# Routing attention rows to eight experts: plain stores in token order and gathers by a table, instead of scatters into expert regions

## The chip, the cores and the metric

The kernel runs on one core of one Trainium2 chip. The core has five engines that run side by side, each with its own instruction queue: TensorE (PE in the profile; PEld is its weight load), VectorE (DVE), ScalarE (ACT), GpSimd (POOL) and SyncE (SP). Transfers between device memory (DRAM) and the on-chip memory are issued from the SP queue or from GpSimd's queue and carried by 16 DMA engines. The metric is device time of one launch in microseconds, lower is better. "The profiled execution" is one launch taken by the hardware profiler; all times of single instructions come from it.

## What is computed

First an attention over 8 batches and 8 heads (576 positions, 64 columns), a sum of a coarse part on positions averaged by four and a narrow local part; then a mixture of 8 experts over the 4608 rows that result, each row going to one expert.

```
out_up = np.repeat(sm_attn(q_d, k_d, v_d), 4, axis=2)     # q_d, k_d, v_d: means over 4 positions
mask = np.abs(pos[:, None] - pos[None, :]) < 4
out_local = softmax(where(mask, scale * q @ k.T, -1e9)) @ v
x = (out_up + out_local) as 4608 rows of 512

logits = x @ w_gate                        # 8 experts
e_idx = np.argmax(logits, axis=1)
gate_w = softmax(logits)[row, e_idx]
eom = sigmoid(x @ w_output_gate)
for e in range(8):
    mask = e_idx == e
    h = np.maximum(x[mask] @ w1[e], 0.0)   # 512 -> 1024
    ye = h @ w2[e]                         # 1024 -> 512
    out[mask] = gate_w[mask, None] * eom[mask, e, None] * ye
```

## The kernel before

**Attention and routing.** A unit is one batch and two heads; there are 32 units (NU), four per batch. Each unit is a set of small tasks: transposes and means of q and k (L382, L389, tasks Tq and Tk), coarse scores (L447, DS), local scores with a mask (L460, L470, LS), means of v (L425, VD), the products with v and the row sums (L493, V1; L503, V2; L515, V3), exponentials and logarithms on ScalarE, and on VectorE and GpSimd the division and the sum that give 128 columns of x, transposed (L538 to L559). TensorE uses its array in several shapes: 64 columns (T, DS), 64 x 64 quarters (LS, V1, V2, V3), 32 columns (VD, L591) and the whole array (L600, L623 to L629, L670).

After each batch, `gate(b)` routes its 576 rows, held as 6 columns (j) of 96 partitions: logits (L591, L600), the maximum and a one-hot of the expert (L610 to L617), the coefficient (L646 to L650), and the rank of the row among those of its expert (L623 to L629, matmuls with a triangular matrix and a running count `cum`). `pos` (L656 to L660) is expert region plus rank. L670 turns x back into rows, L674 copies them into `xh`, where each row also gets its coefficient and its token number (L650, L652). Then GpSimd scatters the rows, six indirect transfers per batch (L679), to row `pos` of `xs_dram`, which has a region of 4608 rows for each expert. The regions' first 640 rows are filled beforehand with a token number out of range (`prefill`, L697, SP queue).

The order of all these tasks on each engine is set by `Plan`: it goes through them with given durations, and among tasks that could start it takes the one with the smallest `10 * slot + AT[kind]`. The order that it gives is the order in the program; the chip then runs each queue in order.

**Experts.** Each expert takes up to 640 rows (CAPJ = 5 blocks of 128). For expert e: one plain load of its region into `xg` (L784, SP queue), 20 transposes (L750) and their evictions (L751), first products with w1 in 64 matmuls of 320 columns (L759, evicted by ScalarE, L762, and VectorE, L764), second products with w2 in 40 matmuls (L769), scaling by the coefficient that stands in the row (L771), and five scatters of 128 rows into `out`, with the token numbers read from the row (L772, GpSimd). xg, xgT, hs and y have two buffers each, the weights three. Weights of experts 0 to 2 are loaded during attention, those of expert 3 and later among the experts (L693, L694, GpSimd, 1 MB each as stored on chip). This part is written expert after expert, and a scheduler of the language puts it in order on each queue.

If an expert has more than 640 rows, a branch at the end (L789) works off the rest.

## Time and profile before

| | us |
|---|---|
| median of 3 runs | 519.19 (516.39 to 520.56) |
| the profiled execution | 523.01 |
| its span, first to last instruction | 520.9 |
| TensorE busy | 419.6 (81%) |
| ScalarE, VectorE, GpSimd busy | 199.2, 187.4, 177.2 |

The span is the time between the first and the last instruction in the profiled execution; about 2 us of that execution lie outside it. A busy share is a mean over stages that differ, so the rows below are taken by stage: attention with routing up to about 320 us, a passage to 342.6 us, the experts up to 510.5 us, and the end. The granted clock (PEclk) is the share of full speed that TensorE was given in a stretch. The page's list of transfers has 48 scatters into hx_xs, 40 into out_dram, eight prefills of 645 KB (5.8 us from issue to landing) and eight loads of xg of 645 KB (4.2 us).

### The profile page before, as it was taken

To read this page: it belongs to the slowest core of one execution; us is meant where nothing else is said; L and a number is where in the kernel's file an instruction comes from. 1 tells how busy PE (TensorE), PEld (TensorE's weight loads), DVE (VectorE), ACT (ScalarE), POOL (GpSimd) and SP (SyncE) were. 2 spreads that over 40 slices of the span, in tenths; PEclk is the share of its full clock that TensorE was granted. 3 is DMA by queue.
4 is the path that set the end of the run, shared out by engine and by line. 5 is a ranking of instruction groups with operands and counts; after the bars stand their busy time and mean duration, and the time that the engine had idled before them with its cause. 6 is when DMAs were issued, how large, how long until landed. Compare 5 with 4: busy or idle time off the path is not lost.

```text
span 520.9 us, 17550 instructions
## 1 busy us (share of the span) xinstructions
PE 419.6 (81%) x7849; PEld 304.6 (58%) x7849; DVE 187.4 (36%) x496; ACT 199.2 (38%) x449; POOL 177.2 (34%) x211
## 2 busy tenths in 40 slices
PE   3787878978897977987997966089959989999991
PEld 2666757656776765765776754065536646566550
DVE  5232443443463462443463453132213313223220
ACT  2243734553563552433463542023313332333331
POOL 6021522535434534424324453405221340512312
PEclk9986986997787895678697886579989997999997
DMA  8998799382992489272212010227893988873202
GB/s 130 178 194 210 172 213 170 75 124 65 173 170 72 80 135 200 53 119 58 60 43 55 18 34 16 78 69 167 133 259 79 202 165 176 198 158 123 91 24 76
DMA packets 85269, 62.74 MB, mean 120 GB/s; under 512 B 49597, under 2 KB 77245, under 8 KB 85184
## 3 DMA queue, kind: packets, MB, share of 16 engines
q0 software_dynamic: 30624, 40.43, 40.6%
q1 hardware_dynamic: 54560, 21.10, 17.9%
q8 instruction: 63, 1.03, 0.8%
q14 instruction: 22, 0.18, 0.1%
HBM read 68.23 MB, written 20.53 MB: 170 GB/s over the span
## 4 chain that ended last, share of the span: by engine, by line
PE 48%; issue 31%; POOL 8%; DMA 4%; ACT 3%; DVE 2%; another core or an unknown queue 2%; POOLq 1%; SPq 0%; DVEq 0%
PE T L389 9%; PE PD L493 7%; POOL out_dram L772 7%; PE T L382 5%; PE PL L515 5%; PE T L425 4%; PE PD L503 4%; PE T L591 3%; PE T L670 3%; DMA qk<-in_k_dram 2%; PE pu L759 2%; PE S L460 2%; PE S L447 2%; PE py L769 1%
## 5 line engine op out<-in xcount | busy, mean ns | idle before, releaser
L759 PE MATMUL pu<-xgT,w 128*128 128x320 f16 x512 | 75.1, 310 | 1.8 <-DVE xgT L751 1.2
L556 POOL TENSOR_TENSOR xT<-xl,xd 128x576 f32<-128x576 f32 x32 | 38.8, 1212 | 102.1 <-DVE xl L549 101.9
L769 PE MATMUL py<-w,hs 128*128 128x512 f16 x320 | 70.4, 379 | 0.0
L679 POOL DMA_INDIRECT hx_xs<-xh,g_pos x48 | 45.1, 939 | 70.1 <-DVE g_pos L660 24.8
L389 PE MATMUL T<-idq,qk 72*64 72x88 f16 (+1 forms) x1024 | 63.0, 312 | 6.3 <-issue 5.9
L759 PEld LDWEIGHTS <-w 128*128 128x128 f16 x512 | 51.8, 101 | 24.5 <-issue 2.9
L772 POOL DMA_INDIRECT out_dram<-y,xg x40 | 39.2, 979 | 64.0 <-ACT y L771 60.2
L762 ACT ACTIVATE hs<-pu 128x320 f16<-128x320 f32 x64 | 28.0, 437 | 83.3 <-PE pu L759 77.7
L389 PEld LDWEIGHTS <-qk 72*64 72x64 f16 x1024 | 47.5, 166 | 9.2 <-issue 9.2
L769 PEld LDWEIGHTS <-hs 128*128 128x128 f16 x320 | 31.3, 98 | 36.4
L764 DVE TENSOR_SCALAR hs<-pu 128x320 f16<-128x320 f32 x64 | 31.4, 491 | 45.7 <-PE pu L759 37.2
L382 PE MATMUL T<-id,qk 72*64 72x72 f16 x1024 | 35.4, 221 | 14.5 <-DMA qk<-in_q_dram 8.9
L493 PE MATMUL PD<-e,vd 64*64 64x72 f32 (+1 forms) x512 | 42.3, 317 | 5.7 <-issue 3.1
L771 ACT ACTIVATE y<-py,xg 128x512 f32<-128x512 f32 x40 | 27.5, 687 | 47.9 <-PE py L769 47.9
L397 DVE COPY kT<-T 128x576 f16<-128x576 f16 x32 | 24.2, 757 | 56.2 <-ACT kd L411 26.5
L493 PE MATMUL PD<-e,on_d 64*64 64x72 f32 (+1 forms) x512 | 42.2, 318 | 2.6 <-issue 2.6
L751 DVE COPY xgT<-tp 128x1024 f16<-128x1024 f16 (+1 forms) x24 | 13.2, 596 | 84.1 <-PE py L769 42.9
L523 ACT ACTIVATE r<-PD 128x582 f32<-128x582 f32 x32 | 21.0, 656 | 57.5 <-PE PD L503 41.6
L397 DVE COPY qT<-T 128x576 f16<-128x576 f16 x32 | 24.2, 757 | 50.9 <-PE T L389 39.2
L493 PEld LDWEIGHTS PD<-e,vd 64*64 64x64 f32 x512 | 36.2, 173 | 9.4 <-issue 8.6
L382 PEld LDWEIGHTS <-qk 72*64 72x64 f16 x1024 | 28.0, 130 | 23.4 <-issue 9.1
L515 PE MATMUL PL<-e,v 64*64 64x57 f32 (+1 forms) x1280 | 33.1, 252 | 10.0 <-issue 9.1
(109 smaller groups left out, 605.8 us busy)
## 6 DMA issues: line engine op xcount, KB each, us to landing
w<-in_moe_w_dram POOLq DMA_DIRECT2D x16, 1024.0 KB
v<-in_v_dram SPq DMA_DIRECT2D x128, 80.0 KB, 4.8
hx_xs<-zt SPq DMA_DIRECT2D x8, 645.0 KB, 5.8
xg<-hx_xs SPq DMA_DIRECT2D x8, 645.0 KB, 4.2
qk<-in_q_dram POOLq DMA_DIRECT2D x7, 576.0 KB
qk<-in_k_dram POOLq DMA_DIRECT2D x7, 576.0 KB
hx_xs<-xh,g_pos POOLq DMA_INDIRECT x48
out_dram<-y,xg POOLq DMA_INDIRECT x40
```

What stands on the lines that cost most here:

```text
L382: nc.tensor.transpose(t16[64 * h:64 * h + 64, HB * c:HB * c + HB], src.tile[:, 2 * hp + h, D * c:D * c + D], id16[0:HB, 0:HB])
L389: nc.tensor.matmul(_ap(o, [o.ap[0], [2, w]]), lhsT=src.tile[:, 2 * hp + h, D * (4 * a + m):D * (4 * a + m) + D], rhs=idq[:, 0:w], start=(a ...
L397: nc.vector.tensor_copy(xT.tile.rearrange("p (n c) -> p n c", c=8), T.tile.bitcast(F16)[:, 0:S].rearrange("p (c n) -> p n c", c=8))
L493: nc.tensor.matmul(p[o:o + 64, h, WC + q0:WC + q0 + c1 - c0], lhsT=w[r, blk, :], rhs=et[r, i, WC + c0:WC + c1], start=(blk == 0), stop=(bl ...
L515: nc.tensor.matmul(p[64 * h:64 * h + 64, par, c0:c1], lhsT=vbuf.tile[r, g, h, :], rhs=et[r, h, c0:c1], start=(g == 0), stop=True, skip_gro ...
L556: nc.gpsimd.tensor_tensor(xT.tile[:, hp, :].rearrange("p (n m) -> p n m", m=4), xl.tile.rearrange("p (n m) -> p n m", m=4), _bc(xd.tile, 4 ...
L679: ins = nc.gpsimd.indirect_dma_start(out=xs_dram.ap(), out_offset=bass.IndirectOffsetOnAxis(ap=pos.tile[:, j:j + 1], axis=0), in_=xh.tile[ ...
L759: nc.tensor.matmul(pu[:, 0:c1 - c0], lhsT=w1sb[:, c, 128 * f:128 * f + 128], rhs=xgT[:, c, c0:c1], start=(c == 0), stop=(c == 3))
L762: nc.scalar.activation(hs[:, f, c0:c1], pu[:, 0:c1 - c0], AF.Relu)
L764: nc.vector.tensor_scalar_max(hs[:, f, c0:c1], pu[:, 0:c1 - c0], 0.0)
L769: nc.tensor.matmul(py, lhsT=hs[:, f, 128 * j:128 * j + 128], rhs=w2sb[:, f, :], start=(f == 0), stop=(f == NG - 1))
L772: ins = nc.gpsimd.indirect_dma_start(out=out_rows, out_offset=bass.IndirectOffsetOnAxis(ap=xgi[:, j, Dm // 2 + 1:Dm // 2 + 2], axis=0), in ...
```

## The change

Rows of x, 514 numbers wide now (512 and the coefficient), are stored in token order, one plain store per batch from the SP queue; the scatters by GpSimd and the prefills are gone. What is to stand where is worked out instead in a table of 128 partitions by 40 columns (8 experts of 5 blocks): VectorE splits `pos` into the lane (low seven bits) and the block, makes a one-hot of each by comparing (`olo`, 128 wide, and `ohi`, 40 wide), multiplies the second by the token number plus one, and six matmuls per batch (task INV) sum the products, so that each token number arrives at its place; VectorE adds that to `acc`, with 576 times the batch added where something arrived. At the end `gidx` is the list to gather by (row 0 where the table is empty) and `sidx` the list to scatter by (out of range where it is empty).

Each expert's rows come by five gathers of 128 rows (GpSimd) into xg, which has three buffers. The experts' part is written in the order in which it is to run: gathers two experts ahead, the transposes for the next expert between the second products of this one, weight loads behind the scatters. The table AT is rewritten, and so are the durations of several tasks and one constant that the plan goes by.

```diff
 AT = {
-    "v": -31.38, "Tq": -3.33, "Tk": 1.99, "evq": -4.73, "evk": 4.65, "qd": -21.49, "kd": -8.83, "VD": 15.17,
+    "v": -56.99, "Tq": -8.95, "Tk": 2.82, "evq": -2.96, "evk": 9.62, "qd": 31.01, "kd": 38.57, "VD": 14.38,
...
-    xs_dram = nc.dram_tensor("hx_xs", (E * REG, XW // 2), I32, kind="Internal")
+    xs_dram = nc.dram_tensor("hx_xs", (N, XW // 2), I32, kind="Internal")
+    gpool = ctx.enter_context(tc.tile_pool(name="gpool", bufs=3))
...
-        tv = add("VD", n, "PE", 0.46, fn, deps=vt + [t_pv], uses=[T, vbuf], mode=32, lat=0.2)
+        tv = add("VD", n, "PE", 0.65, fn, deps=vt + [t_pv], uses=[T, vbuf], mode=32, lat=0.2)
...
-            exti = xh.tile[:, :, Dm:XW].bitcast(I32)
-            nc.vector.tensor_scalar(exti[:, :, 1], tok_i[0:P], scalar1=float(S * b), scalar2=None, op0=ALU.add)
...
-            nc.vector.tensor_scalar(m9.tile, m9.tile, scalar1=1.0, scalar2=float(REG), op0=ALU.subtract, op1=ALU.mult)
-            nc.vector.tensor_tensor(pos.tile, m9.tile, rsel.tile, op=ALU.add)
+            pos = posall[:, b, :]
+            nc.vector.scalar_tensor_tensor(pos, in0=m9.tile, scalar=float(REG), in1=rsel.tile, op0=ALU.mult, op1=ALU.add)
+            nc.vector.tensor_scalar(bk.tile, pos, scalar1=7, scalar2=None, op0=ALU.arith_shift_right)
+            nc.vector.tensor_scalar(lo.tile, pos, scalar1=127, scalar2=None, op0=ALU.bitwise_and)
...
+            nc.vector.tensor_tensor(ohi.tile, _ap(colv, [[colv.ap[0][0], P], [0, NJ], [1, NC]]), _bc(bk.tile, NC),
+                                    op=ALU.is_equal)
+            nc.vector.tensor_tensor(hit.tile, ohi.tile, _bc(tokv[0:P], NC), op=ALU.mult)
...
+            nc.vector.tensor_tensor(olo.tile, _ap(lane, [[lane.ap[0][0], P], [0, NJ], [1, 128]]), _bc(lo.tile, 128),
+                                    op=ALU.is_equal)
...
+            for j in range(NJ):
+                nc.tensor.matmul(G.tile[:, 0:NC], lhsT=olo.tile[:, j, :], rhs=hit.tile[:, j, :], start=(j == 0),
+                                 stop=(j == NJ - 1), skip_group_check=True)
...
+            g = G.tile[:, 0:NC]
+            if b:
+                nc.vector.tensor_scalar(g1.tile, g, scalar1=0.5, scalar2=float(S * b), op0=ALU.is_ge, op1=ALU.mult)
+            nc.vector.tensor_tensor(acc, acc, g, op=ALU.add)
+            if b:
+                nc.vector.tensor_tensor(acc, acc, g1.tile, op=ALU.add)
...
-        for j in range(NJ):
-            def fn(j=j):
-                ins = nc.gpsimd.indirect_dma_start(
-                    out=xs_dram.ap(), out_offset=bass.IndirectOffsetOnAxis(ap=pos.tile[:, j:j + 1], axis=0),
-                    in_=xh.tile[:, j, :].bitcast(I32), in_offset=None, bounds_check=E * REG - 1, oob_is_err=False)
...
+            nc.sync.dma_start(xs_dram.ap()[S * b:S * b + S, :].rearrange("(j p) d -> p j d", p=P),
+                              xh.tile.bitcast(I32))
...
-    for r in range(E):
-        add("pre", 2 * r + 1, "SP", 0.8, lambda r=r: prefill(r), deps=[t_cg])
...
+    def gather(xg, nj, idx, c0):
+        for j in range(nj):
+            nc.gpsimd.indirect_dma_start(
+                out=xg[:, j, :], out_offset=None, in_=xs_dram.ap(),
+                in_offset=bass.IndirectOffsetOnAxis(ap=idx[:, c0 + j:c0 + j + 1], axis=0),
+                bounds_check=N - 1, oob_is_err=False)
...
+        for e in range(E):
+            w1sb, w2sb = wts[e]
+            xgT, hs, y = xts[e]
+            if e + 2 < E:
+                fetch(e + 2)
+            up(xgT, hs, CAPJ, w1sb)
+            if e + 1 < E:
+                xts[e + 1] = tiles(CAPJ)
+            for j in range(CAPJ):
+                col = CAPJ * (E - 1 - e) + j
+                down(xgs[e], hs, y, j, w2sb, sidx[:, col:col + 1], True)
+                if e + 1 < E and 2 * j < CAPJ:
+                    turn(xgs[e + 1], xts[e + 1][0], CAPJ, 2 * j)
+            if e + 3 < E:
+                weights(e + 3)
```

Here `up` is the first products with their evictions, `down` one block's second products with scaling and scatter, `turn` the transposes of two blocks with their eviction, `fetch` five gathers.

What this makes of the queues is seen at three places. GpSimd's queue before, from the last batch's scatters (L679) through experts 0 and 1 (w: weight loads, L772: scatters into out):

```order
L679 DMA hx_xs<-xh_91,g_pos 36864x258 x6
L693 DMA w_7638<-in_moe_w_dram 128x4x1024
L772 DMA out_dram<-y,xg 4608x512 x4
L694 DMA w_7639<-in_moe_w_dram 128x8x512
L772 DMA out_dram<-y,xg 4608x512
L693 DMA w_7834<-in_moe_w_dram 128x4x1024
L772 DMA out_dram<-y,xg 4608x512 x4
```

and after, from the end of attention (L778: gathers, of experts 0 to 2 first, then of 3 and 4; L811: scatters):

```order
L778 DMA xg<-hx_xs,gidx 128x257 x15
L811 DMA out_dram<-y,sidx 4608x512 x5
L730 DMA w_7344<-in_moe_w_dram 128x4x1024
L731 DMA w_7345<-in_moe_w_dram 128x8x512
L778 DMA xg<-hx_xs,gidx 128x257 x5
L811 DMA out_dram<-y,sidx 4608x512 x5
L730 DMA w_7554<-in_moe_w_dram 128x4x1024
```

The loads of w1 moved from ahead of the scatters to behind them, and the gathers now stand in this queue, behind two weight loads. VectorE's queue in the last batch's routing, before, from the second copy of xh on:

```order
L674 COPY xh_91<-T 96x2x512
L646 TENSOR_REDUCE g_se<-g_eg 96x6
L647 TENSOR_SCALAR g_se<-g_se 96x6
L648 SCALAR_TENSOR_TENSOR g_den<-g_ez,g_se 96x6
L650 RECIPROCAL xh_91<-g_den 96x6
L652 TENSOR_SCALAR xh_91<-tok_i 96x6
L656 TENSOR_TENSOR g_rke<-g_oh,T 96x48
L658 TENSOR_REDUCE g_rsel<-g_rke 96x6
L659 TENSOR_SCALAR g_m_6986<-g_m_6986 96x6
L660 TENSOR_TENSOR g_pos<-g_m_6986,g_rsel 96x6
```

and after, from the same copy (now with the third) to the lookup and the coefficient:

```order
L714 COPY xh_100<-T 96x2x512 x2
L668 TENSOR_TENSOR g_rke<-g_oh,T 96x48
L670 TENSOR_REDUCE g_rsel<-g_rke 96x6
L672 SCALAR_TENSOR_TENSOR posall<-g_m_6994,g_rsel 96x6
L673 TENSOR_SCALAR g_bk<-posall 96x6
L674 TENSOR_SCALAR g_lo<-posall 96x6
L684 TENSOR_TENSOR g_olo<-lane,g_lo 96x768
L678 TENSOR_TENSOR g_ohi<-colv,g_bk 96x240
L680 TENSOR_TENSOR g_hit<-g_ohi,tokv 96x240
```

Both copies now stand ahead of the rank (L668), and the coefficient (L660 to L664 of the new file) comes behind these rows. The SP queue before, with the prefills among the loads of v:

```order
L360 DMA v<-in_v_dram 64x5x64 x20
L697 DMA hx_xs<-zt 128x5x258 x2
L360 DMA v<-in_v_dram 64x5x64 x4
L316 DMA wg<-in_moe_w_gate_dram 128x4x8
L317 DMA wg<-in_moe_w_output_gate_dram 128x4x8
```

and after, with the stores of the first two batches (L719):

```order
L373 DMA v<-in_v_dram 64x5x64 x34
L719 DMA hx_xs<-xh_99 96x6x257
L373 DMA v<-in_v_dram 64x5x64 x16
L719 DMA hx_xs<-xh_100 96x6x257
L373 DMA v<-in_v_dram 64x5x64 x16
```

The prefills are gone, and each store stands between loads of v. On TensorE, where the rows are too many to show, neighbouring task groups of different array shape follow each other at 194 places of attention before and at 164 after, the six matmuls of INV counted in.

## Rows read from the trace of the kernel before

**Rows 1.** Stages: us, busy us (instructions) by engine, granted clock, DMA share, GB/s
```profile
18.00:320.00 302.00, 251.00 (x6710) 200.61 (x6707) 129.58 (x345) 139.96 (x336) 114.22 (x124) 0.81 0.59 113
320.00:342.60 22.60, 6.97 (x60) 5.62 (x58) 6.96 (x29) 0.77 (x3) 6.04 (x7) 0.58 0.29 85
342.60:510.50 167.90, 155.37 (x972) 92.99 (x971) 43.29 (x86) 54.77 (x103) 46.71 (x49) 0.95 0.64 141
```

**Rows 2.** Waits in attention: engine line <- releaser: total us, times, longest
```profile
POOL xT L556 <- DVE xl L549: 101.9, 19, 11.6
PE T L425 <- issue: 11.9, 18, 2.4
PEld L460 <- issue: 3.8, 15, 0.7
PE PD L493 <- DVE xd L538: 2.5, 1, 2.5
PE T L425 <- ACT vd L431: 0.2, 1, 0.2
PE T L670 <- issue: 0.2, 1, 0.2
```

**Rows 3.** Timeline of PE: experts 5, 6, 7: start, us, line, [wait before]
```profile
454.38 8.85 PE L759 MATMUL pu<-xgT,w 128*128 128x320 f16 x64 [0.21 <-DMA out_dram<-y,xg]
463.07 8.80 PE L769 MATMUL py<-w,hs 128*128 128x512 f16 x40
471.70 1.06 PE L750 MATMUL tp<-id,xg 128*128 128x128 f16 x16
473.09 0.38 PE L750 MATMUL tp<-id,xg 128*128 128x128 f16 x4 [0.34 <-DVE xgT L751]
473.69 8.85 PE L759 MATMUL pu<-xgT,w 128*128 128x320 f16 x64 [0.21 <-DVE xgT L751]
...
501.69 8.80 PE L769 MATMUL py<-w,hs 128*128 128x512 f16 x40
```

**Rows 4.** Timeline of PE: starts of experts 0, 2 and 4
```profile
342.64 9.86 PE L759 MATMUL pu<-xgT,w 128*128 128x320 f16 x64 [0.21 <-DVE xgT L751]
...
386.62 2.40 PE L750 MATMUL tp<-id,xg 128*128 128x128 f16 x20 [6.17 <-DMA xg<-hx_xs]
...
430.67 2.40 PE L750 MATMUL tp<-id,xg 128*128 128x128 f16 x20 [3.01 <-DMA xg<-hx_xs]
```

**Rows 5.** Waits of the SP queue, all of the span
```profile
SPq L784 <- DMA out_dram<-y,xg: 112.7, 8, 27.9
```

**Rows 6.** Timeline of POOL: weight loads among the scatters of expert 0
```profile
352.80 0.82 POOL L693 DMA_DIRECT2D w<-in_moe_w_dram  x1 [19.16 <-PE pu L759]
...
361.44 0.93 POOL L694 DMA_DIRECT2D w<-in_moe_w_dram  x1
```

**Rows 7.** Stages by 20 us: one of the last experts
```profile
480.00:500.00 20.00, 19.45 (x131) 11.87 (x130) 5.83 (x12) 7.23 (x14) 4.86 (x5) 1.00 0.16 60
```

**Rows 8.** Chain that ended last, 326 to 343 us: start, us, what
```profile
326.15 0.16 DVE g_pos L660
...
332.73 2.37 DMA hx_xs<-xh,g_pos
...
335.69 4.18 DMA xg<-hx_xs
```

**Rows 9.** Timeline 318 to 345 us: rank matmuls, one scatter of rows
```profile
324.93 0.37 PE L626 MATMUL T<-g_oh,ones 96*96 96x40 f16 x5
...
331.51 0.92 POOL L679 DMA_INDIRECT hx_xs<-xh,g_pos  x1 [0.30 <-issue]
```

**Rows 10.** All scatters of L679 and L772: ns shortest/median/longest, first and last start
```profile
L679 POOL DMA_INDIRECT hx_xs<-xh,g_pos x48: 915/921/1050, 88.0 to 332.7; - x48
L772 POOL DMA_INDIRECT out_dram<-y,xg x40: 966/972/1016, 355.8 to 511.5; - x40
```

**Rows 11.** Groups by line and shape: busy us, mean ns
```profile
L545 DVE TENSOR_TENSOR xl<-PL,r 128x570 f32<-128x570 f32 x32 | 24.0, 749 | 0.7
```

More of the change, by code (lines that the diff above doesn't have):

```diff
@@ L70 @@
     SWITCH = 0.13
[L71 removed]
+    NEAR = 0.15
     def __init__(self, at):
@@ L392, in fn @@
                                              skip_group_check=True)
[L393 removed]
+            tp = add("T" + nm, n, "PE", 0.88, fn, deps=loads + [t_id, t_idq], uses=[T, src], mode=64, lat=0.16)
             xT = d[nm + "T"] = Buf(r_qT if i == 0 else r_kT)
@@ L764, in experts @@
                     nc.vector.tensor_scalar_max(hs[:, f, c0:c1], pu[:, 0:c1 - c0], 0.0)
-        y = sbF.tile([128, CAPJ, Dm], F32, tag="y")
-        for j in range(nj):
-            py = psF.tile([128, Dm], F32, tag="Y", bufs=2)
-            for f in range(NG):
-                nc.tensor.matmul(py, lhsT=hs[:, f, 128 * j:128 * j + 128], rhs=w2sb[:, f, :],
-                                 start=(f == 0), stop=(f == NG - 1))
-            nc.scalar.activation(y[:, j, :], py, AF.Copy, scale=coef[:, j, 0:1])
-            ins = nc.gpsimd.indirect_dma_start(
-                out=out_rows, out_offset=bass.IndirectOffsetOnAxis(ap=xgi[:, j, Dm // 2 + 1:Dm // 2 + 2], axis=0),
-                in_=y[:, j, :], in_offset=None, bounds_check=N - 1, oob_is_err=False)
-            if group:
-                tc.declare_no_dep(ins.ins, group="out_scatter", reason="the rows differ")
-                tc.add_to_no_dep_group("out_scatter", ins.ins)
@@ L779, with down @@
-    for e in range(E):
-        if e not in wts:
-            weights(e)
-        base = (E - 1 - e) * REG
-        xg = sbF.tile([128, CAPJ, XW // 2], I32, tag="xg")
-        nc.sync.dma_start(xg, xs_dram.ap()[base:base + 128 * CAPJ, :].rearrange("(j p) d -> p j d", p=128))
-        experts(xg, CAPJ, *wts[e], True)
+    def down(xg, hs, y, j, w2sb, idx, group):
+        py = psF.tile([128, Dm], F32, tag="Y", name="Y", bufs=2)
+        for f in range(NG):
+            nc.tensor.matmul(py, lhsT=hs[:, f, 128 * j:128 * j + 128], rhs=w2sb[:, f, :],
+                             start=(f == 0), stop=(f == NG - 1))
+        nc.scalar.activation(y[:, j, :], py, AF.Copy, scale=xg[:, j, Dm // 2:XW // 2].bitcast(F32))
+        ins = nc.gpsimd.indirect_dma_start(
+            out=out, out_offset=bass.IndirectOffsetOnAxis(ap=idx, axis=0),
+            in_=y[:, j, :], in_offset=None, bounds_check=N - 1, oob_is_err=False)
+        if group:
+            tc.declare_no_dep(ins.ins, group="out_scatter", reason="the rows differ")
+            tc.add_to_no_dep_group("out_scatter", ins.ins)
@@ new lines, in tiles, with fetch @@
+    def tiles(nj):
+        return (sbF.tile([128, 4, 128 * nj], F16, tag="xgT", name="xgT"),
+                sbF.tile([128, NG, 128 * nj], F16, tag="hs", name="hs"),
+                sbF.tile([128, nj, Dm], F32, tag="y", name="y"))
+    with tc.manual_schedule():
+        xgs, xts = {}, {}
+        def fetch(e):
+            xgs[e] = gpool.tile([128, CAPJ, XW // 2], I32, tag="xg", name="xg")
+            gather(xgs[e], CAPJ, gidx, CAPJ * (E - 1 - e))
+        fetch(0)
+        fetch(1)
+        count()
+        xts[0] = tiles(CAPJ)
+        for j0 in range(0, CAPJ, 2):
+            turn(xgs[0], xts[0][0], CAPJ, j0)
+        for e in range(E):
[13 more added lines that the diff above has]
+                weights(e + 3)
```

128 lines of the change are left out of this document (78 added, 50 removed), and 12 rows, old and new, of the table AT.

## The prediction

> **What bounds the kernel now.** The page's first line (TensorE 81% busy) mixes stages, so the first view to read is the table by stage [rows 1]. Up to 320 us (attention, routing) TensorE is busy 251.0 of 302 us at a mean granted clock of 0.81, a mixture of its two levels 1.2 and 2.4 GHz. From 320 to 342.6 us it does 7 us of work in 22.6: the gap between the last head and the first expert. From 342.6 to 510.5 us eight experts run, TensorE busy 155 of 168 us. Then come 10.4 us of last scatter and end of program, up to the span of 520.9, in which nothing is changed.
>
> The second view is what TensorE waited for in attention [rows 2]. Ten of its rows, from 11.9 down to 0.2 us, end with "issue", time with no releaser in the profile; they sum to 41.7 us, and the change adds or removes few matmuls there. Six rows, from 2.5 down to 0.2 us, are waits for another engine's data; they sum to 8.6 us. So a better order can win little by shorter waits for data, and VectorE and GpSimd (129.6 and 114.2 us busy in 302 us, [rows 1]) have room.
>
> The third view is TensorE's timeline among the experts. An undisturbed expert takes 19.31 us [rows 3]: the first products start at 454.38, the second at 463.07 (8.69 later), the next expert's transposes at 471.70 (8.63), its first product at 473.69 (1.99). Three experts are not like that [rows 4]: expert 2 starts after 6.17 us and expert 4 after 3.01 us of waiting for its xg, and after a pause the first products run slower: those of expert 0 show 9.86 us busy, an undisturbed expert's 8.85. Why xg is late stands in the waits of the SP queue [rows 5]: its loads waited 112.7 us for scatters into out_dram, one of them 27.9 us, since a scatter reads its token numbers out of the xg buffer and so holds it until it has landed. On GpSimd's queue the scatters come behind a 1 MB weight load issued early, right after the first products [rows 6].
>
> **The change, part by part.** The sum is made against the profiled execution, 523.01 us; the median of the runs shown is 519.19, 3.8 less, and I take that off at the end.
>
> *Experts.* Three buffers for xg, coefficients taken from xg but token numbers from a constant table (sidx), weight loads behind the scatters, and transposes for the next expert written between the second products. So the two waits go, with the slow clock behind them, and so do the 0.34 and 0.21 us for evictions between transposes and products. What stays per expert is 8.69 + 8.63 and the transposes' own 1.06 + 0.38 = 1.44 us: 18.76 us. Expert 0 still starts after a pause, 9.86 - 8.85 = 1.01 us more, so 19.77; expert 7 has no successor to transpose: 17.32, and 0.17 until its last matmul ends at 510.49. Sum 19.77 + 6 x 18.76 + 17.32 + 0.17 = 149.8 us against 510.49 - 342.64 = 167.85: **18.0 us less**. This needs cover: the next expert's rows must have landed when its transposes come up. Those for expert e+3 are issued when expert e+1 begins, behind two weight loads on the same queue, and the first are wanted one expert and one first product later, 18.8 + 8.7 + 1.7 = 29 us after. The whole stage moves as many bytes as before, and the 16 DMA engines were busy 0.64 of 167.9 us = 107 us [rows 1]; the last experts, which only scatter, show 0.16 x 20 = 3.2 us each [rows 7]. Taking 8 x 3.2 and about 2.5 us for each of seven loads of xg off (an estimate, below its 4.18 us from issue to landing, [rows 8]) leaves some 13 us per pair of weights. So 13 + 2.5 of transfers lie ahead of 29 us: covered, though one period's transfers (13 + 3.2 + 2.5 = 18.7) fill it almost wholly. If the cover is gone, the old waits return; lower bound of the gain about 6 us.
>
> *Gathers instead of one load.* 40 gathers on GpSimd, not measured. Nearest rows are the scatters of rows of the same length, 0.92 us and 0.30 us of issue between them [rows 9], and the wider ones at 0.97 [rows 10]. I take 1.22 us each. Per expert GpSimd then has 5 x 1.22 + 5 x 1.27 + 0.82 + 0.93 = 14.2 of 18.8 us [rows 6, 9, 10]: hidden. Removed with no gain on the path: 48 scatters (48 x 0.92 = 44 us of GpSimd, which stood idle 101.9 us for xl alone, [rows 2, 10]) and eight prefills of 645 KB, which nothing waited for.
>
> *From last head to first product.* Now [rows 8]: routing ends at 326.3, six scatters until 332.73, landing 2.37, load 4.18, transposes, first product at 342.64. After, VectorE makes two copies of xh ahead of the rank instead of one and the small operations of the coefficient behind it, so the rank multiply stays near 325.6. From there: four small operations to the split place, 1.0 us, 326.6; the lookup's three comparisons and products. For those the nearest row is the two-input operation of 570 columns at 749 ns [rows 11], 1.31 ns a column: 768 columns 1.0 us, 240 columns 0.32 us twice, so 328.3. Six small operations at 0.22 finish the coefficient at 329.7, when SP can issue the plain store; meanwhile the six matmuls and the table sum are done by about 330.6, so the store is the later one. Its landing lies between 2.37 (scatter) and 4.18 us (xg load of 645 KB; the store has 592 KB), I take 4.2: gathers from 334.0, the fifth issued at 338.9, landed 341.3 by the scatter's 2.37, four transposes, first product at about 341.9. That is **0.7 us less**; ends -2.5 (store 2.4) and +3 (gathers landing like the xg load, store slower).
>
> *Attention.* VectorE gets per batch 1.0 + 0.63 + 0.16 (place split, one operation folded) + 0.5 (table sum) - 0.16 (token numbers) = 2.1 us, eight times 17 us, on 129.6 of 302 us; TensorE gets eight groups of six narrow matmuls, which by five of the rank matmuls (0.37 us, [rows 9]) cost some 0.5 us a group, 4 us. The rewritten order has 164 instead of 194 places where neighbouring matmul groups use the array in another shape; the nearest row is L460 behind such a place, 3.8 us in 15 = 0.25 us [rows 2], part of which is issue that any place has. Half of it, 0.12 x 30 = 3.7 us, cancels the 4 us. **0**, with ends -12 (all of 30 x 0.25 = 7.5 and the 8.6 us of data waits, less 4) and +10 (half of the additions on the path). The store on SP stands ahead of loads of v for heads some units later, which wait for their buffers longer than for it: 0.
>
> Sum 523.0 - 18.0 - 0.7 + 0 = 504.3; less 3.8: **500.5 us**.
>
> **Rivals.** (1) *Attention shrinks too.* The new order and the freed GpSimd and queues take the -12: 488.5. For it: the waits and shape changes above are real rows. Against: the issue waits dwarf them.
>
> (2) *The lookup lies on the path.* 8 x (2.1 + 0.5) = 21 us back: 521, no change. Against it: VectorE is 57% idle in attention and the lookup's result is needed only at the end.
>
> (3) *Gathers behind weights.* Before, xg came over SP's queue; now it shares GpSimd's with 2 MB of weights per expert. By the Trainium skill, page "DMA: Bandwidth & Descriptors", section "SWDGE vs HWDGE vs iDMA", there is a single queue for transfers that GpSimd issues, and each DMA engine alternates between that one and the one fed by SP. The scatters held back up to 27.9 us [rows 5] look like that; no row here shows a gather behind a weight load. If the share of 18.7 us per period falls short by 3 us in each of the five periods, the queue lags 15 us, more than the 13 us of slack, and pauses of the old size come back from expert 5 or 6 on, 9 us with their clock: 510.
>
> (4) *GpSimd becomes the bound*, the slower case: a gather reads scattered rows of DRAM and might cost more than a scatter. Per expert GpSimd would need 5 x 1.27 + 1.75 = 8.1 us and five gathers; the gain is gone and 1% lost when 8 experts take 173.6 us, 21.7 each, from 2.7 us per gather on. At 3 us: 8 x 23.1 = 185, 536 us. Against: 88 indirect transfers in the trace, of two widths, all take 0.92 to 1.05 us [rows 10].
>
> That the overflow branch is entered can be excluded: the trace has 40 scatters at L772, eight times five, none from a branch, and counts don't change.
>
> **Numbers.** Forecast with its own range 494 to 507: 0.60; (1) 0.17; (3) 0.11; (2) 0.07; (4) 0.05. A measurement here tells about 1% from no change, 5.2 us. Faster (below 514): forecast, (1), (3), about 0.88; same 0.07; slower 0.05. The range leaves out the deeper part of (1), and (2) and (4): 487 to 511.
>
> **What would show it.** In the table by stage of the changed kernel, the experts should take about 150 us at clock 1.00 after the first, an expert 18.8 us on TensorE's timeline with no wait for DMA; a gather's row should read 0.9 to 1.0 us; the first product should start some 22 us after the last head; up to there about 320 us. I am wrong if waits for gathers stand before transposes (3), if GpSimd is over 0.95 busy among the experts (4), or if the last head ends more than 10 us from 320 (1, 2).

## The result and the profile after

The changed kernel takes **483.33 us** (median of 4 runs, 482.45 to 485.67) against 519.88 us before (4 runs, 516.39 to 520.58): ratio 0.930, interval 0.924 to 0.936. The prediction was 500.5 us with a range of 487 to 511. The sign was right, the gain was twice the forecast. Ratios with their intervals, here and below, compare only runs in the faster of two states that a program is seen in, while medians are over all runs, so a ratio is not always the quotient of the medians beside it; the profiled executions of runs a4, d1 and f1 were in the slower state, 4 to 6 us over their medians, and stages read from them are upper bounds.

The table by stage of the changed kernel, cut where its own last head (the end of the last sum on GpSimd that gives columns of x, L569, old L556) and first product lie (columns as in [rows 1]):

```profile
18.00:290.30 272.30, 219.56 (x6675) 182.20 (x6675) 153.88 (x383) 138.36 (x334) 79.41 (x81) 0.86 0.59 106
290.30:313.90 23.60, 8.11 (x67) 5.90 (x68) 9.42 (x37) 0.77 (x3) 7.79 (x8) 0.50 0.22 61
313.90:471.30 157.40, 151.99 (x974) 90.93 (x972) 44.46 (x86) 54.71 (x104) 81.89 (x83) 0.97 0.66 155
```

The last head ends at 290.29 instead of 319.78, the first product starts at 313.90 instead of 342.64, the last product ends at 469.62 instead of 510.49, the span at 481.64 instead of 520.93. So of 39.3 us, **29.5 went in attention**, which was forecast at 0; the passage grew by 0.7, the experts lost 12.1 (forecast 18.0), and the end, from last product to span, grew by 1.6.

What TensorE waits for in the changed kernel's attention, to be read against [rows 2]:

```profile
PE T L402 <- issue: 9.2, 4, 4.4
PE PL L528 <- issue: 6.9, 4, 3.2
PE T L690 <- DVE qT L410: 6.5, 5, 1.6
PE S L483 <- issue: 5.0, 2, 4.4
PE T L605 <- ACT kd L424: 2.2, 3, 0.7
PE T L690 <- DVE g_hit L680: 1.8, 1, 1.8
PE T L438 <- issue: 1.2, 2, 0.7
```

L438 is the old L425, the means of v: its "issue" waits were the largest row of before, 11.9 us in 18, and are now 1.2 in 2. Eight issue rows sum to 33.3 us (41.7 before), nine for data of another engine to 17.4 (8.6 before). All rows together are 50.7 us, 50.3 before: the list of waits shows nothing of the 29.5 us. They are in TensorE's busy time, 219.6 us instead of 251.0 [rows 1] for nearly the same matmuls, at a granted clock of 0.86 instead of 0.81.

The experts, on TensorE's timeline from the fifth transpose group to expert 2:

```profile
313.50 0.61 PE L789 MATMUL T<-id,xg 128*128 128x128 f16 x4 [1.15 <-DMA xg<-hx_xs,gidx]
313.90 6.43 PE L798 MATMUL U<-xgT,w 128*128 128x320 f16 x32
320.92 0.70 PE L798 MATMUL U<-xgT,w 128*128 128x320 f16 x4 [0.59 <-issue]
323.12 0.70 PE L798 MATMUL U<-xgT,w 128*128 128x320 f16 x4 [1.49 <-DVE hs L803]
325.19 1.22 PE L798 MATMUL U<-xgT,w 128*128 128x320 f16 x4 [1.38 <-issue]
326.69 5.20 PE L798 MATMUL U<-xgT,w 128*128 128x320 f16 x20 [0.27 <-DVE hs L803]
...
341.47 8.86 PE L798 MATMUL U<-xgT,w 128*128 128x320 f16 x64
...
359.91 2.34 PE L798 MATMUL U<-xgT,w 128*128 128x320 f16 x16
```

From expert 1 on, each takes 18.44 us with no wait for DMA. Expert 0 takes 27.57: its first products stop three times between 320 and 327 us. The 15 gathers of experts 0 to 2 run until just then on GpSimd (first and last of 15):

```profile
304.85 1.10 POOL L778 DMA_INDIRECT xg<-hx_xs,gidx  x1 [13.83 <-issue]
306.26 1.03 POOL L778 DMA_INDIRECT xg<-hx_xs,gidx  x1 [0.30 <-issue]
...
323.23 1.00 POOL L778 DMA_INDIRECT xg<-hx_xs,gidx  x1 [0.30 <-issue]
```

### The profile page after: what moved, and what is told of

The parts are those of the page before. It is cut to its first block, busy times and chain, and to the rows that moved or that the text cites. A ratio compares the mean times of both kernels' runs of the same rounds, so it can differ in the third digit from the quotient of the medians.

```text
span 481.6 us, 17626 instructions
## 1 busy us (share of the span) xinstructions
PE 388.7 (81%) x7897; PEld 286.8 (60%) x7897; DVE 216.0 (45%) x547; ACT 197.8 (41%) x449; POOL 178.4 (37%) x203
## 4 chain that ended last, share of the span: by engine, by line
PE 58%; DVE 15%; issue 14%; POOL 4%; DMA 3%; ACT 3%; another core or an unknown queue 1%; POOLq 0%; DVEq 0%
PE U L798 12%; PE Y L808 11%; PE T L402 6%; PE PD L506 5%; PE T L395 4%; PE PD L516 3%; PE T L438 3%; PE PL L528 3%; PE T L605 3%; PE T L710 2%; POOL out_dram L811 2%; DVE qT L410 2%; DMA qk<-in_q_dram 2%; DVE kT L410 2%; DVE g_ohi L678 2%
## 5 line engine op out<-in xcount | busy, mean ns | idle before, releaser
L569 POOL TENSOR_TENSOR xT<-xl,xd 128x576 f32<-128x576 f32 x32 | 43.3, 1352 | 127.0 <-DVE xl L562 126.9
L798 PE MATMUL U<-xgT,w 128*128 128x320 f16 x512 | 76.2, 311 | 3.7 <-issue 2.0
L808 PE MATMUL Y<-w,hs 128*128 128x512 f16 x320 | 73.8, 379 | 0.0
L811 POOL DMA_INDIRECT out_dram<-y,sidx x40 | 39.8, 994 | 65.6 <-ACT y L810 38.6
L402 PE MATMUL T<-idq,qk 72*64 72x72 f16 (+1 forms) x1024 | 55.7, 296 | 9.2 <-issue 9.2
L803 DVE TENSOR_SCALAR hs<-U 128x320 f16<-128x320 f32 x64 | 31.4, 492 | 70.3 <-PE U L798 62.4
L801 ACT ACTIVATE hs<-U 128x320 f16<-128x320 f32 x64 | 27.9, 437 | 64.7 <-PE U L798 40.4
L810 ACT ACTIVATE y<-Y,xg 128x512 f32<-128x512 f32 x40 | 27.5, 688 | 56.0 <-PE Y L808 40.6
L778 POOL DMA_INDIRECT xg<-hx_xs,gidx x40 | 40.7, 1016 | 25.7 <-issue 25.1
L395 PE MATMUL T<-id,qk 72*64 72x72 f16 x1024 | 33.4, 213 | 12.1 <-DMA qk<-in_q_dram 8.3
L714 DVE COPY xh<-T 96x1024 f16<-96x1024 f16 x24 | 16.4, 686 | 59.6 <-PE T L710 59.6
L528 PEld LDWEIGHTS PL<-e,v 64*64 64x64 f32 x1280 | 27.6, 151 | 12.5 <-issue 9.1
L541 ACT ACTIVATE r<-PD 64x144 f32<-64x144 f32 x64 | 18.3, 286 | 39.8 <-PE PD L516 39.4
```

Source lines behind the costliest of these rows:

```text
L395: nc.tensor.transpose(t16[64 * h:64 * h + 64, HB * c:HB * c + HB], src.tile[:, 2 * hp + h, D * c:D * c + D], id16[0:HB, 0:HB])
L402: nc.tensor.matmul(_ap(o, [o.ap[0], [2, w]]), lhsT=src.tile[:, 2 * hp + h, D * (4 * a + m):D * (4 * a + m) + D], rhs=idq[:, 0:w], start=(a ...
L528: nc.tensor.matmul(p[64 * h:64 * h + 64, par, c0:c1], lhsT=vbuf.tile[r, g, h, :], rhs=et[r, h, c0:c1], start=(g == 0), stop=True, skip_gro ...
L569: nc.gpsimd.tensor_tensor(xT.tile[:, hp, :].rearrange("p (n m) -> p n m", m=4), xl.tile.rearrange("p (n m) -> p n m", m=4), _bc(xd.tile, 4 ...
L778: nc.gpsimd.indirect_dma_start(out=xg[:, j, :], out_offset=None, in_=xs_dram.ap(), in_offset=bass.IndirectOffsetOnAxis(ap=idx[:, c0 + j:c0 ...
L798: nc.tensor.matmul(pu[:, 0:c1 - c0], lhsT=w1sb[:, c, 128 * f:128 * f + 128], rhs=xgT[:, c, c0:c1], start=(c == 0), stop=(c == 3))
```

## The experiments

Two theories stood first. **Theory 1**: an indirect transfer of GpSimd holds TensorE up while it is under way (called the hold below); taking 48 of them out of attention is the gain. **Theory 2**: the rewritten order made attention shorter. A third came with the second group of runs. The trace of before gave the idea for theory 1. Four scatters of one batch, and TensorE beside them:

```profile
122.71 1.01 POOL L679 DMA_INDIRECT hx_xs<-xh,g_pos  x1 [7.49 <-DVE g_pos L660]
...
126.53 0.92 POOL L679 DMA_INDIRECT hx_xs<-xh,g_pos  x1 [0.30 <-issue]
```

```profile
124.21 0.24 PE L425 MATMUL T<-v,pv 128*32 128x64 f32 x1
124.73 0.30 PE L425 MATMUL T<-v,pv 128*32 128x64 f32 x4 [0.27 <-issue]
125.47 0.33 PE L425 MATMUL T<-v,pv 128*32 128x64 f32 x5 [0.44 <-issue]
126.20 0.45 PE L425 MATMUL T<-v,pv 128*32 128x64 f32 x6 [0.39 <-issue]
126.94 0.45 PE L425 MATMUL T<-v,pv 128*32 128x64 f32 x5 [0.29 <-issue]
128.38 0.42 PE L425 MATMUL T<-v,pv 128*32 128x64 f32 x3 [1.00 <-issue]
```

One group of 24 small matmuls comes in handfuls, one every 0.7 us or so, for more than 4 us. Counted over the 42 scatters ahead of the last head, TensorE starts 24 matmuls per us where no scatter starts within 3 us, and 7.4 between 1.0 and 1.5 us after one has started.

Times of all runs, each median beside that of the kernel before on the same chip. Stages are from the profiled executions: end of the last head; expert 0, first product to first product. Runs a were made on one chip, b and c on a second, d on a third, e and f on a fourth. Which chip the first comparison had is not on record; before took about 520 us there as on the chip of runs a, and "the first chip" below stands for either.

| run | us | before, us | ratio (interval) | last head | expert 0 |
|---|---|---|---|---|---|
| before, after (first comparison) | 483.33 | 519.88 | 0.930 (0.924 to 0.936) | 319.8, 290.3 | 20.3, 27.6 |
| a1 new kernel, old order | 470.91 | 522.61 | 0.899 (0.887 to 0.910) | 277.0 | 27.5 |
| a2 old kernel, new order | 524.28 | 522.61 | 1.008 (1.000 to 1.016) | 318.8 | 20.2 |
| a3 old kernel, no scatters | 458.30 | 522.61 | 0.873 (0.861 to 0.885) | 279.7 | 20.1 |
| a4 new kernel, 48 dummy scatters | 501.91 | 522.61 | 0.952 (0.937 to 0.967) | 314.3 | 26.6 |
| b1 dummies that move no row | 475.99 | 488.92 | 0.975 (0.963 to 0.987) | 291.3 | 21.2 |
| b2 plain dummies | 481.04 | 488.92 | 0.987 (0.978 to 0.995) | 295.1 | 20.6 |
| c1 a1, both fetches held | 461.29 | 488.92 | 0.947 (0.937 to 0.956) | 276.5 | 21.0 |
| c2 a1, second fetch held | 462.57 | 488.92 | 0.948 (0.939 to 0.956) | 279.1 | 20.7 |
| d1 new kernel | 476.25 | 487.81 | 0.985 (0.970 to 1.000) | 296.8 | 20.3 |
| d2 as a1 | 459.88 | 487.81 | 0.951 (0.939 to 0.963) | 277.4 | 20.8 |
| d3 as a4 | 481.02 | 487.81 | 0.990 (0.972 to 1.008) | 296.3 | 20.5 |
| d4 as c1 | 462.83 | 487.81 | 0.962 (0.949 to 0.976) | 276.9 | 19.6 |
| e1 the kernel before | 492.85 | 485.63 | 1.015 (1.004 to 1.025) | 288.0 | 20.8 |
| e2 as b1 | 474.71 | 485.63 | 0.980 (0.971 to 0.990) | 287.4 | 19.6 |
| e3 as c1 | 462.50 | 485.63 | 0.956 (0.947 to 0.966) | 274.9 | 20.2 |
| f1 as b1 | 476.31 | 484.72 | 0.983 (0.974 to 0.992) | 295.1 | 20.4 |
| f2 as c1 | 464.71 | 484.72 | 0.959 (0.949 to 0.969) | 280.7 | 19.9 |
| f3 as a3 | 457.97 | 484.72 | 0.945 (0.927 to 0.962) | 278.1 | 20.1 |

Run e1 is the kernel before itself and came out 1.5% above it, with an interval that leaves out 1: differences below that carry no verdict, whatever their interval.

### Order and scatters apart: a1 to a4

a1 puts the table, durations and constant of before back into the changed kernel; a2 does the reverse.

```diff
-    "id": -60, ..., "qk": 29.31, "v": -56.99, ...
+    "id": -60, ..., "qk": 13.79, "v": -31.38, ..., "hi": 29.84, "lo": 22.45, "INV": 28.26, "acc": 41.41,
...
-    NEAR = 0.15
+    NEAR = 0.2
...
```

> The changed kernel with the old table of slots, the old task durations and the old NEAR constant (the four new kinds of task keep their slots): only the order of attention goes back. Theory 1, indirect transfers issued by GpSimd hold TensorE up in attention (about 0.6 us each, 48 of them): the order matters little, last head ends near 290 us, total 483 to 488. Theory 2, the new order made attention shorter: last head ends near 315 us, total 505 to 512.

> The kernel before with the new table, durations and NEAR: only the order of attention changes, the 48 scatters stay. Theory 1: total 514 to 522, last head near 318 us. Theory 2: last head near 292 us, total 490 to 496.

Measured 470.91 and 524.28 us. The first lies below both theories' ranges, the second above theory 1's by 2 us and 28 us above theory 2's. Theory 2 falls: the new order gives the old kernel nothing, and takes 12.4 us from the new one (483.33 in the first comparison against 470.91, all of it in attention: last head 277.0 against 290.3). TensorE's waits in a1's attention, largest rows:

```profile
PE PL L528 <- issue: 7.6, 6, 2.9
PE T L402 <- issue: 4.7, 3, 3.3
PE PD L506 <- DVE xh L664: 3.5, 1, 3.5
PE T L438 <- issue: 3.4, 2, 2.5
```

All rows together: 26.2 us issue and 9.8 us data, 36.0, against 33.3 and 17.4, 50.7, with the new order. The row T L690 <- DVE qT, 6.5 us, in which the lookup's matmuls stand and the old order has no wait, is the largest part of what grew.

Where that comes from shows in the rows of one operation of the lookup on VectorE (count, then shortest, median and longest in ns), first with the new order, then in a1:

```profile
L678 DVE TENSOR_TENSOR g_ohi<-colv,g_bk x8: 397/1416/1418, 79.1 to 297.9; 96x240 f16<-96x240 int32 x8
```

```profile
L678 DVE TENSOR_TENSOR g_ohi<-colv,g_bk x8: 396/398/404, 85.0 to 284.7; 96x240 f16<-96x240 int32 x8
```

With the new order GpSimd's sum (L569) runs beside it in seven of the eight batches. Each time it takes 1.42 us instead of 0.40 and the product behind it, beside GpSimd's CAST, 0.75 instead of 0.40, while the sum itself takes 1.85 instead of 1.21 us. In the eighth batch, and in all eight of a1, GpSimd runs nothing beside them and the times are the short ones. The old kernel has no lookup, which fits a2, where the new order costs nothing. That this is the whole of the order's loss no run shows.

a3 takes the scatter out of the kernel before:

```diff
-                ins = nc.gpsimd.indirect_dma_start(
-                    out=xs_dram.ap(), out_offset=bass.IndirectOffsetOnAxis(ap=pos.tile[:, j:j + 1], axis=0),
...
+                pass
```

> The kernel before without the 48 scatters of rows (the experts then work on the prefilled rows, which go nowhere; the rest, the prefills and the order of all tasks are as before). Theory 1: last head near 292 us instead of 320, and some 9 us less in the passage, where the last six scatters stood; total 480 to 488. Theory 2: last head stays near 320, only the passage is shorter, total 508 to 513.

Measured 458.30. Its stages:

```profile
18.00:279.70 261.70, 221.84 (x6713) 181.54 (x6713) 132.29 (x345) 139.91 (x336) 74.22 (x81) 0.88 0.63 114
279.70:294.00 14.30, 7.36 (x60) 6.01 (x61) 6.97 (x29) 0.77 (x3) 0.70 (x2) 0.50 0.31 94
294.00:447.20 153.20, 149.31 (x972) 90.00 (x971) 43.13 (x86) 54.80 (x103) 46.53 (x49) 0.99 0.55 96
```

The attention is 40.1 us shorter with the same 6713 or so matmuls, 0.95 us for each of the 42 scatters that lie in it; TensorE's busy time falls from 251 to 222 us and its mean granted clock rises from 0.81 to 0.88. (Passage and experts are shorter too, since no row is stored or written; that says nothing on the change.) More than theory 1 had expected.

a4 adds 48 scatters of the same width from a tile of zeros, into tables that nothing reads, to the changed kernel, three behind every other CAST:

```diff
+            if hp in (1, 3):
+                for j in range(3 * (hp // 2), 3 * (hp // 2) + 3):
+                    ins = nc.gpsimd.indirect_dma_start(
+                        out=dum[b].ap(), out_offset=bass.IndirectOffsetOnAxis(ap=tok_i[0:TB, j:j + 1], axis=0),
+                        in_=dz, in_offset=None, bounds_check=S - 1, oob_is_err=False)
...
```

> The changed kernel with 48 more indirect transfers on GpSimd's queue during attention (six per batch, three behind the second and three behind the fourth cast, 96 rows of 1028 B each from a constant tile to scratch memory that nobody reads); the order of TensorE's work is that of the changed kernel. Theory 1: 48 x 0.6 = 29 us come back, total 505 to 515, and TensorE's matmuls stand 0.6 us apart behind these transfers. Theory 2: 483 to 487.

Measured 501.91, 18.6 us above the changed kernel, 0.39 us a scatter: half of the change's gain is given back by scatters whose result nobody waits for. That is 3 us below what theory 1 expected, but on this chip taking scatters out gains and putting them in costs. The fall of the rate is in these traces too: 1.0 to 1.5 us after a scatter TensorE starts 5.2 matmuls per us in a2 and 9.9 in a4, against 24 and 27 where none starts within 3 us.

### Dummies without rows, plain dummies, held fetches: b1 to c2

b1 is a4 with all indices past the table's end, b2 has plain transfers in their place.

```diff
-   ... IndirectOffsetOnAxis(ap=tok_i[0:TB, j:j + 1], axis=0)   # a4
+   ... IndirectOffsetOnAxis(ap=far, axis=0)                    # b1
+   nc.gpsimd.dma_start(dum[b].ap()[TB * j:TB * j + TB, :], dz) # b2
```

> The changed kernel with the 48 added transfers of run a4, but every index lies past the end of the target, so GpSimd issues them as before and no row moves. Run a4 cost 18.6 us over the changed kernel's 483.3 us, 24.0 us of it in the attention. If the moving rows hold TensorE up: 483 to 488 us and the last ADD near 290 to 294 us. If GpSimd's issue of an indirect transfer holds it up, rows or none: 498 to 505 us and the last ADD near 312 us. A mere delay of GpSimd's own ADD and CAST by the 48 issues would also give 498 to 505 us, and is told apart by run b2.

> The changed kernel with 48 plain transfers from GpSimd in the same places as the dummy scatters of run a4, the same bytes to the same table, no index list. If only indirect transfers hold TensorE up: 484 to 490 us, last ADD near 291 to 296 us. If any transfer that GpSimd issues does, or GpSimd's lost time (about 0.9 us each) delays ADD and CAST: 498 to 505 us.

c1 and c2 are a1 and hold the next experts' gathers back by a small copy on GpSimd that reads an evicted slice of expert 0:

```diff
+            if hook and f == hook[0]:
+                nc.gpsimd.tensor_copy(gate1, hs[:, f - 1, 0:1])
+                hook[1]()
...
-            up(xgT, hs, CAPJ, w1sb)
+            up(xgT, hs, CAPJ, w1sb, (4, lambda: fetch(1)) if e == 0 else None)
...
+            if e == 0:
+                fetch(2)
```

(c1; c2 issues `fetch(1)` ahead as before and has `fetch(2)` in the hook.)

> The changed kernel with the order of before (run a1, 470.9 us), and with the gathers of expert 1 held until the fourth slice of expert 0's first product is evicted and those of expert 2 until expert 0 is done; only expert 0's five gathers are issued ahead. In run a1 expert 0 took 27.5 us and each later one 18.44. If the ten further gathers beside expert 0's first product cost it those 8 us: expert 0 takes 19.5 to 21 us and the whole 462 to 465 us. If expert 0 is slow for another reason (TensorE coming out of 22 us of idle time, its instructions): 27 us and 470 to 472 us.

> As run c1, but the gathers of expert 1 stay ahead of expert 0 and only those of expert 2 are held until the fourth slice. If each gather that runs beside the first product costs its share: about half of c1's gain, expert 0 at 23 to 25 us and the whole at 466 to 468 us. If it is the restart of TensorE alone: 470 to 472 us.

These went to another chip, and there the kernel before took **488.92 us, not 520**. So none of the four settles what it was made for. b1 at 475.99 and b2 at 481.04 show no hold, but on this chip a4 might not either; c1 and c2 are alike, and expert 0 takes 21.2 us in b1 too, with all 15 gathers beside it. What they gave is **theory 3**: whether there is a hold depends on the chip.

### The same on a third chip: d1 to d4

Four kernels again, unedited: the changed kernel, a1, a4 and c1.

> The changed kernel once more. The kernel before took 520 to 523 us on the chip of the first comparison and of runs a1 to a4, and 489 us on the chip of runs b1 to c2; there a dummy kernel with 48 empty scatters kept the attention at 291.3 us and expert 0 at 21.2 us. Theory 3: how much an indirect transfer holds TensorE up belongs to the chip; theory 1 said that it belongs to the kernel. On a chip where before takes about 489 us: theory 3 says 472 to 478 us (ratio 0.965 to 0.98), theory 1 says a ratio of 0.93, 455 us. On a chip where before takes about 520 us both say 483 us.

> The changed kernel with the order of before, again. On a chip where before takes about 520 us: 471 us with expert 0 at 27.5 us, as in run a1. On one where it takes about 489 us: theory 3 says expert 0 near 21 us and 461 to 465 us. The order's part (the changed kernel less this one) was 12.4 us on the first chip; if it is a matter of the order alone, it is 11 to 14 us on either chip.

> The changed kernel with 48 dummy scatters that move rows, again. On a chip where before takes about 520 us: 15 to 20 us above the changed kernel of this comparison, as in run a4. On one where it takes about 489 us: theory 3 says 0 to 5 us above it, theory 1 says 15 to 20 us above it.

> The changed kernel with the order of before and the gathers of experts 1 and 2 held back, again. On a chip where before takes about 520 us: 5 to 8 us below run d2, expert 0 at 20 to 21 us, if the gathers beside the first product are what holds expert 0 there. On one where it takes about 489 us: within 1 us of run d2, since expert 0 has nothing to win.

Before took 487.81 here, and theory 3's numbers came out, but for d2, 1 us below its range: d1 476.25 (ratio 0.985, not 0.93), d3 4.8 us above it with intervals that overlap (18.6 on the first chip), expert 0 at 20 to 21 us in all four. GpSimd is busy 122.4 us in the attention of d3 and 122.6 in that of a4, so it is not that time which costs 18.6 us; and TensorE starts 21 matmuls per us 1.0 to 1.5 us after one, 26 away from them. d4, 462.83, lies 3 us above d2, 459.88, where at most 1 us was expected; the runs of each spread over 6 us. The order's loss stays and is if anything larger: d1 less d2 is 16.4 us by the medians, 14.4 with d1's two slowest runs left out.

### The trace of before on a quiet chip: e1 to f3

e1 is the kernel before, e2 and f1 are b1, e3 and f2 are c1, f3 is a3.

> The kernel before itself, for its trace on this chip. On a chip where it takes about 488 us: theory 3 says that TensorE keeps its rate behind a scatter (no fall from 19 matmuls per us to 7), the last ADD ends near 290 us instead of 319.8 and the experts take 170 to 178 us. If the chip is faster in all stages alike, the last ADD ends near 299 us and the experts take 167 us. On a chip where it takes about 520 us: the trace of the first comparison again, last ADD near 320 us.

> The changed kernel with 48 dummy scatters of which no row moves, again. On a chip where before takes about 520 us: near 502 us as run a4 if GpSimd's issue of an indirect transfer holds TensorE up, near 483 us if the moving rows do. On one where it takes about 488 us: 476 us as in run b1.

> The changed kernel with the order of before and the gathers of experts 1 and 2 held back. On a chip where before takes about 520 us: 462 to 466 us with expert 0 at 20 to 21 us if the ten gathers beside the first product are what made expert 0 take 27.5 us in run a1; 470 us with expert 0 at 27 us if not. On one where it takes about 488 us: 461 to 463 us as in runs c1 and d4.

> The changed kernel with 48 dummy scatters of which no row moves, a third time. On a chip where before takes about 520 us: near 502 us if GpSimd's issue of an indirect transfer holds TensorE up there, near 483 us if the moving rows do. On one where it takes about 488 us: 474 to 477 us, as twice before.

> The changed kernel with the order of before and the gathers of experts 1 and 2 held back. On a chip where before takes about 520 us: 462 to 466 us with expert 0 at 20 to 21 us if the ten gathers beside the first product are what made expert 0 take 27.5 us in run a1; 470 us with expert 0 at 27 us if not. On one where it takes about 488 us: 461 to 463 us, as three times before.

> The kernel before without its 48 scatters, again; the rows of x never reach the table, and the experts' own scatters find no row to write. On a chip where before takes about 520 us: 458 us as in run a3, the last ADD near 280 us. On one where it takes about 488 us theory 3 says that the scatters cost the attention little there: the last ADD at 278 to 288 us against 288.0 in run e1, and 455 to 465 us in all, nearly all of the gain from the store and the waits of the experts that fall away.

A fourth chip, before at 485 us. e2, e3, f1 and f2 repeat the quiet chips' values (474.7 and 476.3; 462.5 and 464.7) and leave open what they would show where the hold exists. e1 carries the verdict. The same batch's four scatters lie in it at 122.13 to 125.95 (first and last of four), and TensorE's means of v come in one piece:

```profile
122.13 1.01 POOL L679 DMA_INDIRECT hx_xs<-xh,g_pos  x1 [10.01 <-DVE g_pos L660]
...
125.95 0.92 POOL L679 DMA_INDIRECT hx_xs<-xh,g_pos  x1 [0.30 <-issue]
```

```profile
123.46 0.54 PE L425 MATMUL T<-v,pv 128*32 128x64 f32 x24
123.93 0.81 PE L515 MATMUL PL<-e,v 64*64 64x60 f32 x40
```

The same 5.7 us from the first scatter on, by windows, before in the first comparison and then in e1:

```profile
122.70:128.40 5.70, 3.31 (x63) 1.88 (x55) 0.85 (x4) 0.66 (x1) 4.75 (x5) 0.81 0.31 81
```

```profile
122.10:127.80 5.70, 5.37 (x224) 4.56 (x216) 3.22 (x9) 3.74 (x10) 4.73 (x5) 1.00 0.33 82
```

GpSimd does the same (4.75 and 4.73 us in five instructions), the transfers move the same (81 and 82 GB/s); TensorE starts 63 matmuls in the one and 224 in the other, far more than the clock's 0.81 and 1.00 could make. Counted over all of e1's scatters, it starts 29 per us 1.0 to 1.5 us after one, 24 to 29 in the 2 us ahead of it, and 23 where none starts within 3 us: no fall. Stages of e1, then of f3, the same without scatters:

```profile
18.00:288.00 270.00, 220.59 (x6713) 181.18 (x6713) 129.22 (x345) 139.71 (x336) 114.01 (x123) 0.90 0.66 126
288.00:310.90 22.90, 7.37 (x60) 6.02 (x61) 7.01 (x29) 0.76 (x3) 6.20 (x7) 0.50 0.28 84
310.90:481.00 170.10, 153.53 (x971) 92.38 (x971) 43.26 (x86) 54.77 (x103) 46.15 (x49) 0.95 0.62 138
```

```profile
18.00:278.10 260.10, 220.20 (x6713) 180.95 (x6713) 132.76 (x345) 139.57 (x336) 74.12 (x81) 0.88 0.64 115
```

Without scatters the two kinds of chip are alike: 458.30 (a3) and 457.97 us (f3), last head 279.7 and 278.1. With them the last head is at 319.8 on the one and at 288.0 on the other. So the scatters of before cost its attention 40.1 us on the first and 9.9 on the fourth; the 30 us between them are the hold, with the lower clock that goes with it. An estimate from the counts agrees: in the stretches up to 2.0 us after a scatter's start, 62 us in all, TensorE starts 734 matmuls in the first trace and 1750 in e1; at 24 per us the 734 are 30 us of work, so some 32 us are lost right there. The 9.9 leans on one execution, 493.19, that is 7.6 us over the median of before beside it, so it may be too high, and the hold then larger. That the chip as a whole is slower is ruled out by the same pair.

## Why the prediction was right or wrong

**Attention, forecast 0, measured -29.5: the step that failed.** On a chip with the hold it adds up from last head to last head, each by one run: scatters out 319.8 to 279.7, -40.1 (a3); stores, lookups and the old order 279.7 to 277.0, -2.7 (a1); the new order 277.0 to 290.3, +13.3. Two statements of the prediction fell. "Removed with no gain on the path: 48 scatters" priced them by the time of the engine that issues them and by who waits for them; nobody does, and yet they set TensorE's pace. And the ten issue rows were taken as fixed, because "the change adds or removes few matmuls there". The largest of them, 11.9 us in 18 at L425 [rows 2], lay beside scatters (16 of the 18 within 2.5 us of a scatter's start), which the timeline of the two engines side by side shows and the list of waits does not. Above all TensorE's busy time, 251.0 us at a clock of 0.81, was taken as work that stays, and some 29 us of it came with the scatters (221.8 in a3, where nothing but the scatters is gone; 219.6 after). The end of -12 that was kept for this term was built from other rows and could not hold it.

**The new order, forecast -3.7 of array shapes against 4 of matmuls.** The sign was wrong: it costs 12.4 us (a1) and 14 to 16 (d1 and d2), and a likely part of that is the lookup on VectorE beside GpSimd's sum, 1.42 us instead of 0.40, which no term of the prediction has. Rival 1 came nearest the time, 488.5, by the wrong mechanism: order and freed queues did not win, and the wins in data waits that it counted are losses (17.4 us instead of 8.6).

**Experts, forecast -18.0, measured -12.1: right in mechanism, one part mis-sized.** Waits for xg are gone. The later experts take 18.44 us, 0.32 less than the 18.76 added up; the last takes 17.49, as forecast. Expert 0 takes 27.57 instead of 19.77: 7.8 - 6 x 0.32 = 5.9 us, the whole miss. On the three quiet chips expert 0 takes 19.6 to 21.2 us with the same 15 gathers (b1, b2, d1 to d3, e2, f1), and from first product to last product's start d1 takes 148.1 us, e1 170.3: there the term holds, and a little more. On the first chip, kernels that have no gathers take 20.1 to 20.3 us for it (before, a2, a3), and those with 15 of them 26.6 to 27.6 (after, a1, a4). There the gathers of the changed kernel run until 324.2, and ScalarE's evictions of expert 0's products come late (every other tile is its):

```profile
317.34 0.44 ACT L801 ACTIVATE hs<-U 128x320 f16<-128x320 f32 x1 [1.57 <-issue]
320.43 0.44 ACT L801 ACTIVATE hs<-U 128x320 f16<-128x320 f32 x1 [2.65 <-PE U L798]
324.70 0.44 ACT L801 ACTIVATE hs<-U 128x320 f16<-128x320 f32 x1 [3.84 <-PE U L798]
326.20 0.77 ACT L801 ACTIVATE hs<-U 128x320 f16<-128x320 f32 x2 [1.06 <-remote]
```

4.27 us lie between two of them where the later experts show 1.09. That it is the same hold is argued from this and from the quiet chips, and not shown: the run that holds the gathers back never met a chip with the hold. Against it stands that between 327 and 471 us, on the same chip, 65 more indirect transfers run beside TensorE, which starts some 7 matmuls per us there, and each expert takes the same 18.44 us as on the quiet chips: so the hold is not a stop beside every indirect transfer.

**Passage, forecast -0.7, measured +0.7.** The gathers start 14.56 us after the last head, forecast 14.2; one follows another by 1.30 to 1.41 us instead of 1.22, and the fifth lands after 3.26 instead of 2.37: 0.3 + 0.5 + 0.9, less 0.2 behind them. Inside the first, the store is issued 9.66 us after the last head (forecast 9.9) and lands in 3.86 (4.2; it has 578 KB in the page's unit, not 592), but the first gather starts 1.04 us after that landing, for which the forecast had 0.1. The ends of -2.5 and +3 held.

**End and median.** From the last product to the end 12.0 us instead of 10.4; the part behind the last transfer's end grew from 5.5 to 7.8, and why is open. The 3.8 us that were taken off for the median belonged to one execution of before; the changed kernel's profiled execution, 483.46, lies at its median.

From the forecast for the profiled execution, 504.3, the misses lead to the measured time: 504.3 - 29.5 + 1.4 + 5.9 + 1.6, and 0.3 less outside the span, is 483.4.

**Rivals (2) to (4).** In the old order the lookup did not lie on the path (a1: 2.7 us below a3's attention, lookups included); in the new one TensorE waits 8.3 us ahead of its matmuls (L690), so (2) has a grain of truth there. GpSimd is 81.9 of 157.4 us busy among the experts, a gather 1.00 us: (4) fell. (3) fell too: between 327 and 471 us TensorE waits 0.3 us in all, none of it for a gather, and the lag that was forecast there stayed inside its cover. By the Trainium skill, page "DMA: Bandwidth & Descriptors", section "SWDGE vs HWDGE vs iDMA", GpSimd's transfers have one queue. The trace does not contradict it: gathers are issued right behind two weight loads.

**What the change is worth, then.** The changed kernel itself was timed on one quiet chip: 11.6 us less by the medians, but a ratio of 0.985 (0.970 to 1.000), which is about 7 us and no more than what parts e1 from the same kernel beside it. The parts, taken from several quiet chips, have that sign and size: experts 22 less, scatters 9.9 less (e1 and f3), the order 14 to 16 more, passage and end some 3 more, 12 to 15 less; each rests on single executions that can be some 7 us off, so that they meet is in part luck. The changed kernel with the order of before beats both everywhere that it ran: 470.91 (ratio 0.899) and 459.88 us (0.951); holding the fetches back adds nothing on a quiet chip.

**Open.** Why the first chip has the hold and three do not, and whether it is the chip or what state it was in at the time (the chip of runs a was used in one session); whether the issue of an indirect transfer or its moving rows hold TensorE up there (b1 met only quiet chips), whether held fetches give expert 0 its 7 us back there; and why the hold is not seen beside the later experts.

## To carry to other kernels

An instruction that nobody waits for can still be dear, and a long busy time need not be all work: before such an instruction is priced at nothing, lay the timeline of the engine that issues it beside that of the busiest engine and count what the latter starts per us with and without it. Waits named "issue" are not a constant of the code, so ask what else runs when they are long. Take a rewritten order apart from the rest of its change, and run a kernel whose gain is a surprise on another chip, where 0.93 can turn into 0.985.

## What had not been expected of the hardware

- On one chip TensorE started 7.4 matmuls per us instead of 24 between 1.0 and 1.5 us after an indirect transfer of GpSimd; on another, with the same program, 29 and no fall. In all, the same program took 520 us on the one and 485 to 493 on three others, and 458 on both kinds once the scatters were out.
- Plain transfers from GpSimd (q, k and weights) showed no such fall even where the hold exists: 26 matmuls per us 1.0 to 1.5 us after one, over the 18 of them in the attention of the first trace of before.
- A gather of 128 rows of 1028 bytes takes GpSimd 1.00 us and follows the one before by 1.30; landing takes 3.3 us.
- A comparison on VectorE took 1.42 us beside a sum on GpSimd and 0.40 without it, and the sum 1.85 instead of 1.21; seven times in the changed kernel, and again in d1.
